# A recurrence with a highway layer on one core: bv by channel halves, weights scaled on ScalarE, a shorter ramp, and a new list of all operations

## The chip, the cores and the metric

The kernel runs on one core of a Trainium2 chip. That core has five engines with their own instruction queues: TensorE (PE, with PEld for its weight loads), VectorE (DVE), ScalarE (ACT), GpSimd (POOL) and SyncE (SP), which here issues the transfers. 16 DMA engines move data between the chip's main memory and the on-chip buffers. The metric is device time in microseconds, the median of several executions. The profile describes one execution, and its times count from the start of that execution's span.

## The reference

The input has 4 sequences of 6336 tokens with 256 channels, 25344 tokens in all. A gated recurrence over time is followed by a highway layer with two 256x256 weights:

```python
sig = 1.0 / (1.0 + np.exp(-f_logit))
f = lower_bound + (1.0 - lower_bound) * sig
i = 1.0 - f
for t in range(S):                      # per sequence
    h = f[:, t] * h + i[:, t] * x[:, t]
    y[:, t] = h
H = np.maximum(y @ w_h, 0.0)
T = 1.0 / (1.0 + np.exp(-(y @ w_t + b_t)))
out = T * H + (1.0 - T) * y
```

All data come and go as float32: 52 MB are read and 26 MB written.

## The kernel before

The tokens are cut into 28 units, in blocks of 128 tokens: two units of 2 blocks, one of 4, twenty-three of 8, one of 4 and one of 2. Each unit goes through these steps; a letter names each step in the list of operations, with the unit's number and a part behind it (`s4.1` is the scan of unit 4, channel half 1), a `v` puts the step on VectorE that else runs on ScalarE or GpSimd, and a number after a colon is the buffer it takes.

- `l` and `x` load the gate's logits and the input (SP issues them).
- `u` makes 1 - sigmoid of the logits on ScalarE (L256), with tokens on partitions.
- `b` multiplies u and x into `bv`, mostly on GpSimd (L264). A piece covers two block pairs and all 256 channels, so a unit of 8 blocks has two pieces of 1024 elements per partition.
- `i` and `p` turn u and bv with TensorE so that channels stand on partitions (uT at L271, bT at L291), once for each half of 128 channels.
- `f` scales uT into the gate (L282 on ScalarE, L280 on VectorE), and `s` is the scan over the tokens on VectorE (L308): y = f*y + bT, in which each unit goes on from the last token of the one before.
- `z` and `g` are the two weight products (L320 and L114), `t` the sigmoid on ScalarE (L333), `d` a combination of g and y on VectorE (L337), `e` the product d*t on GpSimd or VectorE (L343).
- `o` turns y and d back and adds them on TensorE (L365, L366), `c` copies the result out of the accumulator (L378 on ScalarE, L376 on VectorE) and `w` stores it.

The signs are arranged so that y is kept scaled by a constant per channel; the weights are multiplied by that constant `cc` once, in the ramp, and an identity is taken off w_h. In the kernel before VectorE does all this (`WT` at L217, `WH` at L231 and L233), with a negated scaled identity, `ndiag` (L212), that it makes first. `k` steps are filler matmuls on zeros, mostly in the ramp.

What sets the order is the list itself: it is walked once, each step's instructions are appended to the queue of their engine, and they stay in that order there. Buffers are taken by the number in the list: five accumulator tiles, four output tiles, and rings for l, x, u, bv, f, y, d and t. Loads and stores stand in one queue, SP's, and a store that waits for its copy holds back the loads behind it. `shared` adds a wait: a GpSimd product waits for the VectorE product (or the VectorE constant work) that stands ahead of it in the list.

Of the kernel before, what the change touches and what calls it, by code (L numbers as in the profile page):

```python
# [19 lines left out]
def kernel(  # L20
# [21 lines left out]
    parts = [2] * 2 + [4] + [8] * 23 + [4] + [2]  # L42
    units, at = [], 0
    for n, nb in enumerate(parts):
        units.append((nb, at, {2: (0, 1), 4: (0, 1, 2), 8: (0, 2, 4)}[nb], (0, 2048) if 7 <= n <= 21 else {2: (0, 256, 512), 4: (0, 512, 1024), 8: (0, 1024, 1536, 2048)}[nb]))
# [4 lines left out]
k*3:1 i0.1:0 f0.1:0 dg i1.0:1 b1.0v:1 f1.0:1 k*3:1 k*3:a0 p0.1:1 s0.1:0 i0.0:0 u2:0 f0.0v:0 p0.0:1 s0.0 x6:1 l7:2  # L50
k*3:a0 WT pb:0 k*3:a1 i2.0:0 p1.0:1 f2.0:0 WH k*3:1 s1.0:1 i2.1:0 b2.1v:0 g0.0:1 b2.0 i1.1:1 z0.1:2 f2.1:1 cb f1.1v:2
z0.0:0 g0.1:a0 p1.1:1 t0.0:0 d0.0:0 k*3:1 d0.1 p2.0:0 s1.1 k*3:0 e0.0v z1.1:1 p2.1:1 t0.1 u3:0 l8:3 g1.1:0 x7:2 s2.0:2
e0.1 d1.1:1 b3.0:0 z1.0:2 t1.0:0 i3.1:0 f3.1:0 o0.0:0 g1.0:2 c0.0:0 s2.1 d1.0 b3.1v g2.1:2 i3.0:0 d2.1:0 p3.1*3:1 t1.1
e1.1 e1.0 k*2:0 w0.0 u4:1 z2.0:1 f3.0:1 z2.1:0 b4.0:1 s3.1:0 p3.0:0 o1.0:2 t2.1:0 u27:0 b4.1 c1.0:1 s3.0 w1.0 x8:3
i4.0:1 g2.0:0 f4.0:0 d2.0 i4.1:1 p4.0:0 l9:1 x9:4 l11:4 t2.0 u5:2 e2.1v e2.0v z3.0:0 g3.1:1 b27.0:0 z3.1:2 s4.0:1
p4.1:0 f4.1:1 i5.0:1 t3.0:0 t3.1 d3.1:1 b5.0:2 g3.0:0 f5.0:0 s4.1 o2.0:1 u6:1 b5.1 c2.0:2 d3.0 w2.0 i5.1:1 x11:0 e3.2
g4.1:2 p5.0:0 d4.1:0 b6.0:1 f5.1:1 s5.0:2 z4.1:0 t4.1:1 p5.1:1 b6.1 u7:2 e3.1 s5.1 l10:0 z4.0:1 t4.0 g4.0:0 i6.0:0
e3.0v p6.0:1 d4.0 o3.0:1 e4.2 b7.0:2 f6.0:0 s6.0:3 e4.0v i6.1:0 b7.1 u8:3 f6.1:1 o3.1:0 c3.0:0 c3.1:1 w3.1 w3.0 g5.0:2
# [15 lines left out]
p15.1:1 s15.1 c12.1:1 b17.1:2 f16.0:2 z14.1:0 z14.0:2 p16.0:0 s16.0:1 c12.0:3 t14.1:1 t14.0 g14.0:1 d14.0 i16.1:1
w11.1 l19:1 u18:3 x18:0 b17.0 e14.0 g15.1:0 d15.1:2 z15.0:2 i17.1:0 x19:3 f16.1:0 b18.0:3 p16.1:1 f17.1:1 b18.1 l20:2
s16.1 o13.1:1 t15.0:0 p17.0:0 g15.0:0 w12.1 d15.0 c13.1:0 u19:1 b19.1:1 o13.0:2 p17.1:1 z15.1:1 c13.0:2 z16.0:0
s17.1:2 t15.1 t16.0:1 z16.1:2 s17.0 g16.0:1 w13.1 t16.1 i18.0:1 d16.0:0 g16.1:0 o14.0:2 i18.1:0 f18.0:0 d16.1 e15.0v
o14.1:1 p18.0:1 s18.0:3 u20:2 w12.0 z17.0:0 c14.0:0 c14.1:1 f18.1:1 g17.0:2 d17.0:1 z17.1:1 b19.0 t17.0:0 i19.1:0
f19.1:0 p18.1:1 o15.1:0 w13.0 s18.1 t17.1 x20:1 i19.0:0 l21:0 g17.1:2 e16.0 d17.1 o15.0:1 f19.0:2 b20.0:2 b20.1
p19.1:0 x21:2 w14.0 i20.1:1 c15.1:2 g18.1:0 w14.1 s19.1:0 c15.0:3 z18.0:1 f20.1:1 l22:1 o16.0:2 d18.1:2 w15.1 u21:1  # L80
t18.0:1 p19.0:0 c16.0:0 i20.0:1 g18.0:0 s19.0 f20.0:0 o16.1:1 c16.1:1 z18.1:2 i21.1:0 b21.1:1 p20.0:1 t18.1 e17.0v
d18.0 o17.0:1 w15.0 z19.1:0 b21.0 f21.1:2 g19.0:2 s20.0:1 x22:0 d19.0:0 p20.1:0 s20.1 c17.0:2 t19.1:0 o17.1:1 u22:2
e18.0 z19.0:0 g19.1:2 b22.1:2 c17.1:3 t19.0 i21.0:1 d19.1 e19.0 i22.0:0 b22.0 f21.0:0 g20.1:1 z20.1:0 l23:2 w16.0
# [12 lines left out]
t27.0:1 o25.3:1 d26.1 g27.0:a0 w23.1 z27.1:a1 w24.1 w24.0 e26.0 c25.2:0 e26.1v o26.0:2 o26.1:0 d27.0:0 g27.1:a0 d27.1
w25.0 c25.3 t27.1 e27.0 e27.1v o27.0:1 c27.0v:1 c26.0:2 o27.1:a0 c26.1 w25.1 w26.0 w27.0 c27.1:3 w27.1
# [110 lines left out]

    def do_dg(slot):
        for h in range(NH):  # L210
            pin(nc.vector.tensor_scalar(diag[:, h], ident_h, cc[:, h:h + 1], None, op0=ALU.mult))
            last = pin(nc.vector.tensor_scalar(ndiag[:, h], ident_h, ncc[:, h:h + 1], None, op0=ALU.mult))  # L212
        shared(last, False)

    def do_WT(slot):
        for h in range(NH):
            last = pin(nc.vector.tensor_scalar(w_sb[:, 1, h], w_raw[:, 1, h], cc[:, h:h + 1], None, op0=ALU.mult))  # L217
# [83 lines left out]
    def half(n, key, h):  # L301
        return st[n][key][:, h * tokens(n):(h + 1) * tokens(n)]
# [120 lines left out]
```

## Time and profile before

| what | us |
|---|---|
| median of 3 runs | 208.47 |
| lowest and highest | 208.37, 209.25 |
| span of the profiled execution | 206.1 |
| VectorE busy | 194.5 |
| TensorE busy | 192.6 |
| ScalarE busy | 191.9 |
| GpSimd busy | 173.8 |
| first bv on VectorE | 5.52 |
| first bv on GpSimd | 12.91 |

The span is the profiled execution's own time; the runs are timed around it, which accounts for the 2.4 us between the span and the median. Busy time is the sum of an engine's instructions, overlaps counted once; waiting and issuing do not count. A row of the timeline gives start, duration, engine, line, operation, the tiles written and read, the number of instructions merged into the row (x2), and in brackets the idle time ahead of it with what ended it. In the rows of groups the mean duration of one instruction stands in ns.

### The profile page before, as it was taken

The page shows a single profiled execution, that of the slowest core. Times are in us where ns is not written, and L with a number is a line of the kernel's source. Part 1 is how long each engine was busy: PE and PEld are TensorE (multiplying, and loading weights), DVE is VectorE, ACT ScalarE, POOL GpSimd, SP SyncE. Part 2 cuts the span into 40 slices and gives each one's busy share as a digit, 9 for nine tenths or more (in the row PEclk, how much of TensorE's full clock was granted, in tenths as well). Part 3 has the DMA queues.
Part 4 walks back from the last instruction along what each step waited for, and adds up shares of the span by engine and source line. Part 5 has one row for each costly group of instructions (what it writes and reads, how often), then busy time and mean ns, then how long its engine had stood idle before and what let it go on. Part 6 is the DMA issues. An engine that isn't in the chain of part 4 may idle for free.

```text
span 206.1 us, 4635 instructions
## 1 busy us (share of the span) xinstructions
PE 192.6 (93%) x1837; PEld 133.8 (65%) x1837; DVE 194.5 (94%) x159; ACT 191.9 (93%) x192; POOL 173.8 (84%) x93
## 2 busy tenths in 40 slices
PE   7798799799998999999999999999999999999991
PEld 2366465566685776676577576677758758776770
DVE  0899999999999999999899999999999999999972
ACT  4369999999999999999999999999999999999891
POOL 3036989789979997999999999799899999998840
PEclk9999999999999999999999999999999999999997
DMA  6999999999999999999999999999999999725396
GB/s 196 370 424 422 411 418 423 409 423 417 414 423 408 429 417 426 423 420 413 425 424 416 433 411 417 429 415 418 407 422 422 414 392 378 286 104 204 138 382 248
DMA packets 16125, 78.68 MB, mean 382 GB/s; under 512 B 1764, under 2 KB 2536, under 8 KB 10216
## 3 DMA queue, kind: packets, MB, share of 16 engines
q1 hardware_dynamic: 16096, 78.39, 93.6%
q8 instruction: 14, 0.23, 0.4%
q14 instruction: 7, 0.06, 0.1%
q10 hardware_dynamic: 8, 0.00, 0.0%
HBM read 52.43 MB, written 25.95 MB: 380 GB/s over the span
## 4 chain that ended last, share of the span: by engine, by line
PE 53%; ACT 14%; DMA 13%; DVE 10%; issue 6%; POOL 2%; SPq 1%; ACTq 0%; DVEq 0%; POOLq 0%
DMA x<-in_x_dram 9%; DVE y L308 8%; PE op L366 7%; PE bT L291 7%; PE op L365 7%; PE g L320 7%; PE z L320 6%; PE uT L271 6%; PE g L114 6%; PE z L114 6%; ACT o L378 4%; ACT f L282 4%; DMA out_dram<-o 4%; ACT t L333 3%; POOL bv L264 2%
## 5 line engine op out<-in xcount | busy, mean ns | idle before, releaser
L264 POOL TENSOR_TENSOR bv<-u,x 128x1024 bf16<-128x1024 f16 (+1 forms) x49 | 100.9, 2085 | 16.9 <-DVE bt L207 10.7
L308 DVE TENSOR_TENSOR_SCAN y<-f,y,bT 128x1024 bf16<-128x1024 f16 (+5 forms) x54 | 106.8, 1989 | 0.2 <-PE bT L291 0.2
L343 POOL TENSOR_TENSOR d<-d,t 128x512 bf16<-128x512 bf16 (+3 forms) x33 | 73.3, 2234 | 9.6 <-DVE d L343 4.2
L337 DVE SCALAR_TENSOR_TENSOR d<-y,ncc,g 128x1024 bf16<-128x1024 bf16 (+2 forms) x56 | 63.1, 1137 | 1.5 <-PE g L320 1.0
L333 ACT ACTIVATE t<-z,bt 128x1024 bf16<-128x1024 f32 (+2 forms) x56 | 58.9, 1088 | 1.3 <-PE z L114 0.7
L282 ACT ACTIVATE f<-uT,ncc 128x1024 f16<-128x1024 f16 (+2 forms) x51 | 55.4, 1098 | 3.4 <-PE uT L271 2.2
L378 ACT COPY o<-op 128x1024 f32<-128x1024 f32 (+2 forms) x55 | 52.1, 984 | 2.4 <-PE op L366 1.6
L256 ACT ACTIVATE u<-l 128x2048 f16<-128x2048 f32 (+2 forms) x28 | 49.8, 1781 | 2.8 <-DMA l<-in_f_logit_dram 2.7
L366 PE MATMUL op<-ident_b,d 128*128 128x128 bf16 x396 | 49.5, 219 | 0.6 <-DVE d L343 0.6
L365 PE MATMUL op<-diag,y 128*128 128x128 f16 x396 | 49.7, 219 | 0.1
L366 PEld LDWEIGHTS <-d 128*128 128x128 bf16 x396 | 44.0, 113 | 3.2 <-DVE d L343 0.7
L365 PEld LDWEIGHTS <-y 128*128 128x128 bf16 x396 | 44.2, 113 | 1.7
L320 PE MATMUL g<-y,w_sb 128*128 128x512 bf16 (+1 forms) x112 | 39.5, 367 | 0.9 <-DVE d L337 0.7
L320 PE MATMUL z<-y,w_sb 128*128 128x512 bf16 (+1 forms) x112 | 39.3, 367 | 0.4 <-ACT o L378 0.4
L291 PE MATMUL bT<-ident_f,bv 128*128 128x128 f32 x198 | 31.8, 277 | 4.3 <-DVE y L308 2.6
L114 PE MATMUL z<-y,w_sb 128*128 128x512 bf16 x92 | 34.9, 379 | 0.0
L114 PE MATMUL g<-y,w_sb 128*128 128x512 bf16 x92 | 34.9, 379 | 0.0
L320 PEld LDWEIGHTS <-w_sb 128*128 128x128 f16 x224 | 21.6, 98 | 17.5 <-issue 0.9
L271 PEld LDWEIGHTS <-u 128*128 128x128 f16 x396 | 26.3, 98 | 10.2 <-issue 2.6
L271 PE MATMUL uT<-ident_h,u 128*128 128x128 f16 x396 | 31.2, 220 | 1.6 <-DVE y L308 0.8
L291 PEld LDWEIGHTS bT<-ident_f,bv 128*128 128x128 f32 x198 | 22.4, 141 | 12.3 <-ACT f L282 3.0
L114 PEld LDWEIGHTS <-w_sb 128*128 128x128 f16 x184 | 18.0, 98 | 16.7 <-issue 1.8
(39 smaller groups left out, 58.7 us busy)
## 6 DMA issues: line engine op xcount, KB each, us to landing
out_dram<-o SPq DMA_DIRECT2D x48, 512.0 KB, 7.7
l<-in_f_logit_dram SPq DMA_DIRECT2D x23, 1024.0 KB, 12.0
x<-in_x_dram SPq DMA_DIRECT2D x23, 1024.0 KB, 13.4
l<-in_f_logit_dram SPq DMA_DIRECT2D x2, 512.0 KB, 7.5
x<-in_x_dram SPq DMA_DIRECT2D x2, 512.0 KB, 7.2
l<-in_f_logit_dram SPq DMA_DIRECT2D x3, 256.0 KB, 2.9
x<-in_x_dram SPq DMA_DIRECT2D x3, 256.0 KB, 3.9
out_dram<-o SPq DMA_DIRECT2D x2, 256.0 KB, 16.3
```

The lines of the kernel that those rows point to most:

```text
L114: return pe.add_instruction(mybir.InstMatmult(name=nc.get_next_instruction_name(), start_tensor_calc=start, stop_tensor_calc=stop, tile_si ...
L264: shared(pin(e.tensor_mul(st[n]["bv"][:, a:c].rearrange("p k d j -> p k j d"), st[n]["u"][:, 2 * a:2 * c].rearrange("p (k j) d -> p k j d" ...
L271: pin(nc.tensor.transpose(uT[:, j * P:(j + 1) * P], st[n]["u"][:, j, h * P:(h + 1) * P], ident_h))
L282: pin(nc.scalar.activation(to, of, AF.Identity, scale=ncc[:, h:h + 1], bias=1.0))
L291: pin(nc.tensor.transpose(words[:, k:k + g * (P - 1) + 1:g], pair, ident_f))
L308: pin(nc.vector.tensor_tensor_scan(y[:, c:e], st[n]["f", h][:, c:e], st[n]["bT", h][:, c:e], 0.0 if fresh else carry[h], op0=ALU.mult, op1 ...
L320: pin(nc.tensor.matmul(p[:, a:e], w, half(n, "y", ki)[:, a:e], start=ki == 0, stop=ki == NH - 1))
L333: pin(nc.scalar.activation(half(n, "t", m), st[n]["z", m][:, :tokens(n)], AF.Sigmoid, bias=bt[:, m:m + 1]))
L337: pin(nc.vector.scalar_tensor_tensor(half(n, "d", m), half(n, "y", m), ncc[:, m:m + 1], st[n]["g", m][:, :tokens(n)], op0=ALU.mult, op1=AL ...
L343: shared(pin(e.tensor_mul(st[n]["d"][:, a:c], st[n]["d"][:, a:c], st[n]["t"][:, a:c])), not eng)
L365: pin(nc.tensor.matmul(o, half(n, "y", h)[:, cols], diag[:, h], start=True, stop=False))
L366: pin(nc.tensor.matmul(o, half(n, "d", h)[:, cols], ident_b, start=False, stop=True))
```

## The change

The units are cut anew: two of 2 blocks, three of 4, twenty-two of 8, one of 4, one of 2, which is 29. A piece of bv now covers one channel half and all blocks of its unit, in a tile of its own, so that the turning of that half waits for that piece alone. y has a tile for each half, from a ring of eight. In the ramp GpSimd subtracts the identity from w_h in place (`IW`), and ScalarE scales both weights (`WHa`, `WTa`, two instructions of 256 elements each); `ndiag` is gone. The list of all operations is new from the first token to the last.

```diff
-    parts = [2] * 2 + [4] + [8] * 23 + [4] + [2]
+    parts = [2] * 2 + [4] * 3 + [8] * 22 + [4] + [2]
...
-l1:0 l0:1 x0:0 x1:1 k*3:a0 l2:2 wt wh x2:2 l3:3 x3:3 l4:4 pc:0 x4:4 u0:0 l27:1 l5:5 b0.0v:0 x27:0 x5:5 u1:1 cc l6:0
+l0:0 k*3:a0 x0:0 k*2:0 pc:0 k*3:1 l1:1 wh wt u0:0 x1:1 u1:1 l2:2 l3:3 b0.1v:0 b0.0v:1 cc dg k*2:a0 i0.0:1 i0.1:0 f0.1:0
...
+    def do_IW(slot):
+        for h in range(NH):
+            own = w_raw[:, 0, h, h * P:(h + 1) * P]
+            last = pin(nc.gpsimd.tensor_sub(own, own, ident_f))
+        shared(last, True)
...
-            pin(nc.vector.tensor_scalar(diag[:, h], ident_h, cc[:, h:h + 1], None, op0=ALU.mult))
-            last = pin(nc.vector.tensor_scalar(ndiag[:, h], ident_h, ncc[:, h:h + 1], None, op0=ALU.mult))
+            last = pin(nc.vector.tensor_scalar(diag[:, h], ident_h, cc[:, h:h + 1], None, op0=ALU.mult))
...
+    def scaled(k, act):
+        for h in range(NH):
+            if act:
+                pin(nc.scalar.activation(w_sb[:, k, h], w_raw[:, k, h], AF.Copy, scale=cc[:, h:h + 1]))
...
-    def do_b(n, k, eng, slot):
-        if "bv" not in st[n]:
-            st[n]["bv"] = sb([P, NB // 2, D, 2], BF16, "bv", slot)
-        a, c = units[n][2][k:k + 2]
+    def do_b(n, h, eng, slot):
+        nb = units[n][0]
+        bv = sb([P, NB // 2, P, 2], BF16, "bv", slot)
+        own = slice(h * P, (h + 1) * P)
         e = nc.vector if eng else nc.gpsimd
-        shared(pin(e.tensor_mul(st[n]["bv"][:, a:c].rearrange("p k d j -> p k j d"),
-                                st[n]["u"][:, 2 * a:2 * c].rearrange("p (k j) d -> p k j d", j=2),
-                                st[n]["x"][:, 2 * a:2 * c].rearrange("p (k j) d -> p k j d", j=2))), not eng)
+        shared(pin(e.tensor_mul(bv[:, :nb // 2].rearrange("p k d j -> p k j d"),
+                                st[n]["u"][:, :nb, own].rearrange("p (k j) d -> p k j d", j=2),
+                                st[n]["x"][:, :nb, own].rearrange("p (k j) d -> p k j d", j=2))), not eng)
+        st[n]["bv", h] = bv
...
     def do_s(n, h, eng, slot):
-        flat(n, "y", "y", slot)
+        st[n]["y", h] = sb([P, NB * P], BF16, "y", slot)
```

The list shows at three places in the ramp what it moves. First VectorE's queue from its first bv on, before:

```order
L264 TENSOR_TENSOR bv<-u,x 128x2x256
L200 TENSOR_SCALAR ncc<-lbT 128x2
L201 TENSOR_SCALAR cc<-lbT 128x2
L211 TENSOR_SCALAR diag<-ident_h,cc 128x128
L212 TENSOR_SCALAR ndiag<-ident_h,ncc 128x128
L211 TENSOR_SCALAR diag<-ident_h,cc 128x128
L212 TENSOR_SCALAR ndiag<-ident_h,ncc 128x128
L264 TENSOR_TENSOR bv<-u,x 128x2x256
L308 SCALAR_TENSOR_TENSOR y<-f,bT 128x256
L280 TENSOR_SCALAR f<-uT,ncc 128x256
L308 SCALAR_TENSOR_TENSOR y<-f,bT 128x256
L217 TENSOR_SCALAR w_sb<-w_raw,cc 128x256 x2
```

The same place after the change (the scan is named by its form, y is what it writes):

```order
L276 TENSOR_TENSOR bv<-u,x 128x2x128 x2
L200 TENSOR_SCALAR ncc<-lbT 128x2
L201 TENSOR_SCALAR cc<-lbT 128x2
L217 TENSOR_SCALAR diag<-ident_h,cc 128x128 x2
L293 TENSOR_SCALAR f<-uT,ncc 128x256
L323 SCALAR_TENSOR_TENSOR y<-f,bT 128x256 x2
L293 TENSOR_SCALAR f<-uT,ncc 128x256
L207 COPY bt<-tbT 128x2
L276 TENSOR_TENSOR bv<-u,x 128x2x128
L352 SCALAR_TENSOR_TENSOR d<-y,ncc,g 128x256
```

The products of bv are half as wide, ndiag and the weights are gone, and the first d stands where the weights stood. ScalarE's queue in the ramp, before:

```order
L256 ACTIVATE u<-l 128x512 x2
L282 ACTIVATE f<-uT,ncc 128x256 x2
L256 ACTIVATE u<-l 128x1024
L282 ACTIVATE f<-uT,ncc 128x512 x2
L333 ACTIVATE t<-z,bt 128x256 x2
L256 ACTIVATE u<-l 128x2048
```

and after:

```order
L268 ACTIVATE u<-l 128x512 x2
L295 ACTIVATE f<-uT,ncc 128x256
L228 ACTIVATE w_sb<-w_raw,cc 128x256 x4
L295 ACTIVATE f<-uT,ncc 128x256
L348 ACTIVATE t<-z,bt 128x256
L268 ACTIVATE u<-l 128x1024
```

The four scalings of the weights stand between the first two f that ScalarE makes. SP's queue from the start, before (l is the logits, x the input, w_raw the two weights as they come):

```order
L244 DMA l<-in_f_logit_dram 128x512 x2
L244 DMA x<-in_x_dram 128x512 x2
L244 DMA l<-in_f_logit_dram 128x1024
L187 DMA w_raw<-in_moe_w_t_dram 128x2x256
L190 DMA w_raw<-in_moe_w_h_dram 128x2x256
L244 DMA x<-in_x_dram 128x1024
```

and after:

```order
L256 DMA l<-in_f_logit_dram 128x512
L256 DMA x<-in_x_dram 128x512
L256 DMA l<-in_f_logit_dram 128x512
L190 DMA w_raw<-in_moe_w_h_dram 128x2x256
L187 DMA w_raw<-in_moe_w_t_dram 128x2x256
L256 DMA x<-in_x_dram 128x512
```

x of unit 0 moves from third to second place, both weights move ahead of x of unit 1, and w_h comes ahead of w_t. Later in the list loads use rings of six buffers throughout, where before l used three and x four after the ramp, and one of the four output tiles keeps its store from unit 17 until unit 25.

More of the change, by code (lines that the diff above doesn't have):

```diff
@@ L54 @@
[L54 to L58, printed above, removed]
@@ L74 @@
[L74 to L78, printed above, removed]
@@ L79 @@
[L79 to L83, printed above, removed]
@@ new lines @@
+p15.1:0 i16.0:1 e13.0 f16.0:2 d14.0:2 w12.1 g14.1:1 o12.0:2 s15.1:1 d14.1 u17:3 w11.1 i16.1:1 b16.1:0 p16.0:0 s16.0:6 f16.1:0
+b17.0:2 c12.0:3 z14.0:0 t14.0 b17.1:3 e14.0 o13.0:1 p16.1:1 c13.0:2 o13.1:2 l19:2 c13.1:0 s16.1:7 i17.0:0 g15.1:0 x18:0
+z15.0:1 p17.0:1 f17.0:1 d15.1:1 w10.0 z16.0:2 i17.1:0 g16.1:0 s17.0:2 w13.1 l20:3 x19:1 w12.0 t15.0:2 t16.0:1 g15.0:1 z15.1:2
+d16.1:0 g16.0:0 p17.1:1 d15.0 f17.1:2 b18.0:5 u19:0 b18.1:4 d16.0 i19.0:0 t15.1 o14.1:1 z16.1:2 s17.1:3 f19.0:0 c14.1:1 t16.1
```

119 lines of the change are left out of this document (66 added, 53 removed).

## The prediction

> **What bounds the kernel now.** I read the busy totals first, then a table of stages, then the timelines of the ramp. The page's busy times:
>
> ```profile
> span 206.1 us, 4635 instructions
> PE 192.6 (93%) x1837; PEld 133.8 (65%) x1837; DVE 194.5 (94%) x159; ACT 191.9 (93%) x192; POOL 173.8 (84%) x93
> ```
>
> Nothing stands out: three engines are within two percent of each other. The table of stages says where the missing 6% lies:
>
> ```profile
> 0.00:12.00 12.00, 9.76 (x40) 4.13 (x41) 6.40 (x19) 5.27 (x8) 1.62 (x11) 1.00 0.86 303
> 12.00:32.00 20.00, 18.03 (x160) 12.12 (x160) 20.00 (x23) 19.07 (x21) 14.94 (x11) 1.00 1.02 419
> 32.00:172.00 140.00, 135.19 (x1324) 95.77 (x1323) 139.43 (x93) 139.58 (x129) 132.87 (x58) 1.00 1.02 417
> 172.00:190.00 18.00, 18.00 (x179) 12.66 (x177) 18.00 (x12) 17.30 (x20) 17.31 (x11) 1.00 0.61 242
> 190.00:206.10 16.10, 11.63 (x143) 9.10 (x140) 10.66 (x16) 10.68 (x18) 7.01 (x6) 0.94 0.63 246
> ```
>
> The columns are PE, PEld, DVE, ACT and POOL busy, the granted clock, the DMA share and GB/s. From 32 to 172 us VectorE lacks 0.57 us of 140 and ScalarE 0.42. So the program lasts as long as VectorE's head start (when its dense work begins), plus its work, plus the drain. The DMA engines are full there too, but the share falls to 0.61 after 172 us, when the loads are over and the engines are not, so I take them as a constraint on the order and not as the end. What a new list can win in the middle is half a microsecond; the ramp and the drain are where time can go.
>
> VectorE's ramp before, from its timeline (start, duration, line, form, idle before):
>
> ```profile
> 5.52 0.73 DVE L264 TENSOR_TENSOR bv<-u,x 128x512 bf16<-128x512 f16 x1 [4.39 <-DMA x<-in_x_dram]
> ...
> 6.99 0.28 DVE L212 TENSOR_SCALAR ndiag<-ident_h,ncc 128x128 f32<-128x128 f16 x1
> ...
> 9.86 0.59 DVE L217 TENSOR_SCALAR w_sb<-w_raw,cc 128x256 f16<-128x256 f32 x2
> 10.36 0.35 DVE L231 SCALAR_TENSOR_TENSOR w_sb<-w_raw,cc,ndiag 128x128 f16<-128x128 f32 x1
> 10.62 0.28 DVE L233 TENSOR_SCALAR w_sb<-w_raw,cc 128x128 f16<-128x128 f32 x1
> ...
> 12.06 0.71 DVE L264 TENSOR_TENSOR bv<-u,x 128x512 bf16<-128x512 f16 x1
> 12.67 0.14 DVE L207 COPY bt<-tbT 128x2 f32<-128x2 f32 x1
> 12.73 0.47 DVE L280 TENSOR_SCALAR f<-uT,ncc 128x256 f16<-128x256 f16 x1
> 13.12 0.89 DVE L337 SCALAR_TENSOR_TENSOR d<-y,ncc,g 128x256 bf16<-128x256 bf16 x2
> 13.94 0.74 DVE L308 TENSOR_TENSOR_SCAN y<-f,y,bT 128x256 bf16<-128x256 f16 x1
> 14.59 0.27 DVE L343 TENSOR_TENSOR d<-d,t 128x256 bf16<-128x256 bf16 x1
> ...
> 16.40 1.27 DVE L308 TENSOR_TENSOR_SCAN y<-f,y,bT 128x512 bf16<-128x512 f16 x1
> 17.59 0.46 DVE L337 SCALAR_TENSOR_TENSOR d<-y,ncc,g 128x256 bf16<-128x256 bf16 x1
> 17.96 1.75 DVE L264 TENSOR_TENSOR bv<-u,x 128x1024 bf16<-128x1024 f16 x1
> ...
> 24.83 0.72 DVE L337 SCALAR_TENSOR_TENSOR d<-y,ncc,g 128x512 bf16<-128x512 bf16 x1
> 25.47 0.78 DVE L343 TENSOR_TENSOR d<-d,t 128x512 bf16<-128x512 bf16 x2
> 26.17 2.34 DVE L308 TENSOR_TENSOR_SCAN y<-f,y,bT 128x1024 bf16<-128x1024 f16 x1
> 28.43 1.25 DVE L337 SCALAR_TENSOR_TENSOR d<-y,ncc,g 128x1024 bf16<-128x1024 bf16 x1
> 29.61 2.34 DVE L308 TENSOR_TENSOR_SCAN y<-f,y,bT 128x1024 bf16<-128x1024 f16 x1
> 31.86 1.25 DVE L337 SCALAR_TENSOR_TENSOR d<-y,ncc,g 128x1024 bf16<-128x1024 bf16 x1
> ```
>
> Records overlap by some 0.08 us, so I count start to start: scans 0.65, 1.19 and 2.26 us for 256, 512 and 1024 tokens; d 0.37, 0.64 and 1.18; e 0.19 and 0.35 (256, 512); f of 256 0.39; a bv of 512 elements 0.61 (12.06 to 12.67). At 31.86 us the scans of units 0 to 4, 3072 tokens, are done.
>
> **The change, part by part.** Arrival of data first. The chain of waits gives two landings by transfer, ScalarE's timeline two more:
>
> ```profile
> 1.63 3.79 DMA x<-in_x_dram
> 6.82 14.43 DMA x<-in_x_dram
> ```
>
> ```profile
> 4.12 1.15 ACT L256 ACTIVATE u<-l 128x512 f16<-128x512 f32 x2 [1.27 <-DMA l<-in_f_logit_dram]
> 6.39 0.84 ACT L282 ACTIVATE f<-uT,ncc 128x256 f16<-128x256 f16 x2 [1.12 <-DVE cc L201]
> 8.67 1.06 ACT L256 ACTIVATE u<-l 128x1024 f16<-128x1024 f32 x1 [1.44 <-DMA l<-in_f_logit_dram]
> 11.22 0.69 ACT L282 ACTIVATE f<-uT,ncc 128x512 f16<-128x512 f16 x1 [1.49 <-PE uT L271]
> ```
>
> One transfer queue serves SP's order, so arrival goes by bytes: 0.52 MB (two pieces of 256 KB) by 4.1 us, 0.79 by 5.4, 1.57 by 8.6, 6.82 (x of unit 4) by 21.25; the last two make 5.25 MB in 12.6 us, 416 GB/s. In the new SP order x0 is second (4.1), l1 third (5.4), wh (1.05 MB) by 6.5 and wt by 7.5 (between the rows), x1 at 8.6, later than before since both weights now stand ahead of it; l2 9.9, l3 11.1, x2 12.4, x3 13.7, x4 16.2, x5 21.25.
>
> VectorE then walks so. The first bv starts at 4.2 and not 5.52 us: minus 1.3. The two halves of unit 0 (256 elements each; between half of 0.61 and all of it; I take 0.33, as the rows scale with size), ncc, cc, two diag and f0.0 end at 5.9. The scan s0.1 needs f0.1, which on ScalarE stands behind the u of unit 1 (5.4 plus 0.57, half of the x2 row) and takes 0.42: 6.5, a new wait of 0.6. Two scans and f1.0 end at 8.25; bv of unit 1 waits for x1 until 8.6, 0.35 more. From there bv, d0.1, bv, s1.1, e, s1.0, d0.0, an f of 512 (0.65, between 0.39 and the 1.2 of twice its size and d's rate), e and d1.0 reach 12.7, two bv of unit 2 13.9. Then come six scans of 512 (7.1), d of 256 and three of 512 (2.3), e's of units 1 to 3 (1.4) and s5.1: 27.0. What they wait for is there: GpSimd makes the four bv of units 3 and 4 from 13.9 to 18.7 at 1.2 each, and s5.1, at 24.8, needs x5 (21.25) and one bv of 2.2. d4.1 and s5.0 end at 29.9, with a tenth for hand-overs at 30.0, where the same 3072 tokens stood at 31.86: **1.8 us earlier**. The parts: 1.3 from the start; 0.2 less work on VectorE (the weights and ndiag, 2x0.28 + 0.59 + 2x0.35 + 2x0.28 less overlap, leave, 1.8; three more e, more bv pieces, split scans and the f of 512 come back); 0.9 of new waits against it; the remaining 1.2 is what stood idle or blocked in the ramp before.
>
> ScalarE takes four weight scalings. None is in the trace; 256 elements of f take 0.42 and 512 of u 0.57, so 0.28 to 0.42 each, 0.33 taken, 1.3 us in all. They lie between f0.1 (6.4) and f1.1, where ScalarE before waited 1.12, 1.44 and 1.49 us in three places, so they cost nothing unless that cover goes. Ahead of the first stand wh and GpSimd's two subtractions of 128 elements, some 0.4 each (below the 0.67 of 256), done at 7.3; its w_sb follows at 7.7, g0.1 at 8.2, before VectorE asks for it at 8.9. If this ran 0.7 later, d0.1 would be late next.
>
> GpSimd's rows, by form:
>
> ```profile
> L264 POOL TENSOR_TENSOR bv<-u,x 128x1024 bf16<-128x1024 f16 x45 | 96.2, 2165 | 5.4 <-DVE d L343 3.0 <-PE bT L291 1.3 <-DMA x<-in_x_dram 0.9
> L343 POOL TENSOR_TENSOR d<-d,t 128x1024 bf16<-128x1024 bf16 x2 | 4.3, 2155 | 0.7 <-DVE d L343 0.7
> L264 POOL TENSOR_TENSOR bv<-u,x 128x512 bf16<-128x512 f16 x4 | 4.7, 1192 | 11.5 <-DVE bt L207 10.7 <-DVE d L343 0.8
> L343 POOL TENSOR_TENSOR d<-d,t 128x256 bf16<-128x256 bf16 x4 | 2.6, 672 | 4.0 <-DVE d L337 1.8 <-DVE bv L264 1.3 <-DVE d L343 0.9
> ```
>
> A bv by channel half has eight runs of 128 elements instead of four of 256. Four runs cost 2165 and one run (the d row) 2155 ns, so a run is nearly free: 44 more such instructions at zero to 10 ns extra, taken as nothing. Its other bound is that each run costs what an instruction does at its start, 2x1192 - 2165 = 219 ns, a rival below. What it gives: the first half's transposes wait for one GpSimd instruction and not for two, 2.1 us less latency, which buys slack and no busy time. The y tiles by halves only free buffers sooner. TensorE loses six filler matmuls; it has gaps, nothing follows.
>
> After the point reached both lists hold the same VectorE work: 21 units of eight blocks, one of four, one of two, three f of 1024, two copies, and 14 e's (more of 512) for 13: within 0.1 us by the rows. ScalarE, too, has the same u, f, t and o of those units left. Middle and drain I price at nothing, between a gain of 2 us and a loss of 3 (below). The sum: span 206.1 - 1.8 = 204.3 us. The median of 208.47 stands 2.4 above the profiled span, hence **206.7 us**.
>
> **Rivals.** (1) The list also closes what is left: 0.57 us in the middle, and of the 5.4 us that VectorE is idle after 190 us perhaps 1.3. That makes 204.9. For it: the halves give slack; against: the drain's steps are the same chain of small units.
>
> (2) ScalarE gives the gain back. It is as dense as VectorE from 32 us on; if u's wait for data as long as before, its 1.3 us of scaling come on top: 208.0.
>
> (3) Slower: VectorE collides with GpSimd. The bv row at 17.96 takes 1.75 us where two of 0.61 would do, because GpSimd was in an instruction:
>
> ```profile
> 16.40 2.14 POOL L264 TENSOR_TENSOR bv<-u,x 128x1024 bf16<-128x1024 f16 x1 [0.72 <-DMA x<-in_x_dram]
> ```
>
> This ends at 18.54; 1.2 us later is 19.7, just when the VectorE row ends. So VectorE stood still some 0.5 us. VectorE now has 27 products of two such operands (bv and e) for 20. Seven more at 0.5 us are 3.5: 210.2. It decides from 0.4 us each on. Against it: the list makes GpSimd wait for the VectorE product ahead of it, and the e rows above ran at 0.35 and 0.19, unblocked. The Trainium skill (SBUF — State Buffer, "Who interferes with whom") says that a VectorE instruction with two SBUF inputs and a GpSimd instruction that reads SBUF exclude each other, and that the one issued first keeps the port to its end; by that rule, which this pair of rows bears out, the worst case is a whole GpSimd instruction per product.
>
> (4) Slower: each run of the new bv costs a start on GpSimd, up to 4 x 0.22 = 0.88 us an instruction. Of GpSimd's 32 idle us, 10.4 lie in the first row of the stages and 9.1 in the last; the other 12.8 allow 0.29 us for each of the 44. Above that it decides: at 0.5 us GpSimd lengthens the span by 22 - 12.8 = 9 us, 215.9. The pair 2165 and 2155 speaks against it.
>
> (5) Slower: stores. One of four output tiles is held from unit 17 to unit 25, so three turn over while a store takes
>
> ```profile
> out_dram<-o SPq DMA_DIRECT2D x48, 512.0 KB, 7.7
> ```
>
> 7.7 us to land. A copy that waits stops ScalarE; 3 us in all make 209.7, and from 2.8 on it is slower. Against it: a unit, with two stores, is 2x2.26 + 2x1.18 = 6.9 us of VectorE, so three tiles turn over in 10.
>
> **How the numbers follow.** Forecast 0.50 (its own range 205.4 to 207.9), rival 1 0.12, rival 2 0.16, rival 3 0.11, rival 4 0.06, rival 5 0.05. Half a percent, 1.04 us, is about what a measurement of this kernel can tell from no change: 207.43 and 209.51 are the marks. Faster is 0.45 of the forecast and rival 1, 0.57; same 0.05 of the forecast and most of rival 2, 0.19; the rest is slower, 0.24. The range from 204.4 to 210.2 leaves out rival 4, half of rival 3 and the far ends.
>
> **What would show it.** Right: VectorE's first bv near 4.2 us, the scans of 3072 tokens done near 30.1, weight rows on ScalarE near 7 us, GpSimd's bv at 2.16 us, 0.5 to 1 us idle on VectorE between 32 and 172 us. Wrong: bv rows on GpSimd over 2.3 us, e or bv rows on VectorE far over their size, copies that wait for stores, or VectorE idle over 2 us in the middle.

## The result and the profile after

The kernel after takes 218.46 us in the median of 4 runs (217.48 to 219.46), the kernel before beside it 208.86 (208.37 to 210.78). The ratio is 1.0455, with a 95% interval of 1.0392 to 1.0517: 9.6 us slower, where 206.7 was forecast and 210.2 was the end of the range. The ratios leave out single executions that fell in a slower state, so a ratio can differ a little from that of the medians given beside it. The experiments below were measured in three groups on two chips, each group beside runs of the kernel before (208.31, 208.16 and 208.30 us), and every ratio is against those.

The page after, busy times:

```profile
span 217.7 us, 4632 instructions
PE 195.3 (90%) x1803; PEld 134.3 (62%) x1831; DVE 195.8 (90%) x163; ACT 194.5 (89%) x200; POOL 176.6 (81%) x98
```

The span is 11.6 us longer, 2 us more than the medians differ, because the profiled execution is the slowest of the four (219.46). VectorE works 195.8 us where it worked 194.5, so it idles 21.9 us where it idled 11.6: 10.3 of the 11.6 us are waits, 1.3 are more busy time. The table of stages, with the columns of the prediction's, says when:

```profile
0.00:12.00 12.00, 10.47 (x50) 4.74 (x50) 6.62 (x19) 7.40 (x14) 2.48 (x13) 1.00 0.82 302
12.00:32.00 20.00, 18.18 (x146) 11.20 (x148) 19.84 (x26) 18.82 (x24) 13.25 (x9) 1.00 1.02 420
32.00:172.00 140.00, 127.90 (x1235) 90.91 (x1253) 133.03 (x89) 130.66 (x119) 125.00 (x55) 0.99 0.98 379
172.00:190.00 18.00, 15.73 (x132) 10.32 (x133) 14.34 (x10) 16.39 (x16) 14.71 (x7) 0.91 0.92 358
190.00:217.70 27.70, 22.97 (x252) 17.14 (x252) 21.98 (x23) 21.19 (x31) 21.16 (x17) 0.99 0.67 258
```

From 32 to 172 us VectorE lacks 6.97 us (before 0.57), and the last column falls from 417 to 379 GB/s. Between 172 and 190 us, where before the loads were over, transfers still run at 358.

The ramp did become shorter. Its end on VectorE's timeline after:

```profile
28.67 2.35 DVE L323 TENSOR_TENSOR_SCAN y<-f,y,bT 128x1024 bf16<-128x1024 f16 x1 [0.16 <-PE bT L304]
30.93 1.38 DVE L352 SCALAR_TENSOR_TENSOR d<-y,ncc,g 128x512 bf16<-128x512 bf16 x2
```

At 30.93 us the scans of 3072 tokens are done, which before was at 31.86. By the ends of the later scans, which the two lists place differently between the other steps, the lead is not lost for good until 114 us: 6144 tokens are done 1.6 us later than before, 7168 tokens 3.6 us earlier, 14336 tokens 1.1 us earlier (113.9 against 114.9), but 15360 tokens 5.7 us later (127.5 against 121.8) and 18432 tokens 8.0 us later.

**Where it went.** The page's row of GB/s in forty equal slices, before:

```profile
GB/s 196 370 424 422 411 418 423 409 423 417 414 423 408 429 417 426 423 420 413 425 424 416 433 411 417 429 415 418 407 422 422 414 392 378 286 104 204 138 382 248
```

and after:

```profile
GB/s 193 384 425 417 420 420 419 413 422 353 286 318 425 427 416 423 372 420 387 319 422 362 324 358 280 357 425 420 424 356 320 425 398 347 271 290 112 366 264 277
```

Before, the transfers stand at 407 to 433 GB/s for thirty slices in a row; after, the same height is broken from the tenth slice (49 us) on. Two wide windows of the same columns as the stages put numbers on it, before:

```profile
10.00:50.00 40.00, 36.07 (x313) 23.91 (x313) 39.97 (x40) 37.76 (x38) 31.18 (x20) 1.00 1.02 418
50.00:140.00 90.00, 87.62 (x870) 62.32 (x868) 89.43 (x60) 89.58 (x83) 85.79 (x36) 1.00 1.02 420
```

after:

```profile
10.00:50.00 40.00, 37.16 (x318) 23.78 (x321) 39.84 (x44) 38.82 (x43) 30.05 (x18) 1.00 1.02 419
50.00:140.00 90.00, 81.83 (x789) 58.44 (x800) 84.98 (x55) 83.17 (x77) 78.86 (x34) 0.98 0.97 366
```

Until 50 us both move the same. From 50 to 140 us the kernel after moves 90 x 0.366 = 32.9 MB where before it was 37.8; the missing 4.9 MB take 11.6 us at 420 GB/s, which is as much as the span grew. That is a hint and not a proof: in this window VectorE itself loses only 4.5 us against before, and the other waits come later. The experiments have to show the cause.

Why the transfers ran dry shows SP's queue after (start, duration, line, what is issued):

```profile
39.34 0.34 SPq L397 DMA_DIRECT2D out_dram<-o  x1
39.79 0.87 SPq L256 DMA_DIRECT2D x<-in_x_dram  x1
41.80 0.33 SPq L256 DMA_DIRECT2D l<-in_f_logit_dram  x1
54.73 0.34 SPq L397 DMA_DIRECT2D out_dram<-o  x1
55.17 0.38 SPq L256 DMA_DIRECT2D x<-in_x_dram  x1
55.60 0.79 SPq L256 DMA_DIRECT2D l<-in_f_logit_dram  x1
```

By the list, the issues from 39.34 on are w4.0, x10, l12, w5.0, x11 and l13. SP stands 12.6 us in front of the store of unit 5, whose copy is not made yet (11.6 of them are put down to that copy), and with it stand x11 and l13, whose buffers are free. What was queued before lands meanwhile (l12 at 55.43), and the slices 353, 286 and 318 follow. There are more such holds, at 72, 119, 147 and 166 us, 9 to 12 us each. How much SP waits in all is no sign of it. Its waits for copies before (in total, times, longest):

```profile
SPq L382 <- ACT o L378: 110.2, 37, 7.5
```

and after:

```profile
SPq L397 <- ACT o L393: 113.6, 30, 11.6
```

The sums are alike; single holds grew longer, and loads with free buffers stand behind them. The bill comes later, as waits for data that land at the last moment. The waits after, by engine (in total, times, longest; two views, ScalarE's and GpSimd's):

```profile
ACT u L268 <- DMA l<-in_f_logit_dram: 8.0, 6, 2.4
ACT o L393 <- DMA out_dram<-o: 3.2, 3, 2.7
```

```profile
POOL bv L276 <- DMA x<-in_x_dram: 7.7, 8, 1.9
```

The same three were 2.7, 0.4 and 0.9 us before. VectorE sees them one or two steps on. Its longest wait after, and ahead of it on ScalarE's timeline a copy that waits for a store:

```profile
111.54 2.35 DVE L323 TENSOR_TENSOR_SCAN y<-f,y,bT 128x1024 bf16<-128x1024 f16 x1 [0.51 <-PE bT L304]
117.66 1.28 DVE L352 SCALAR_TENSOR_TENSOR d<-y,ncc,g 128x1024 bf16<-128x1024 bf16 x1 [3.77 <-PE g L115]
```

```profile
112.73 1.01 ACT L393 COPY o<-op 128x1024 f32<-128x1024 f32 x1 [2.72 <-DMA out_dram<-o]
113.64 1.12 ACT L348 ACTIVATE t<-z,bt 128x1024 bf16<-128x1024 f32 x1
```

The chain of waits after has the store (start, duration):

```profile
99.80 12.91 DMA out_dram<-o
```

It was issued at 99.80 and landed at 112.71, and with it the output tile came free; the copy freed the accumulator, TensorE's g followed, and d with it. So the row names TensorE, and the cause is a transfer three steps back.

### The profile page after: what moved, and what is told of

Same layout as the page of the kernel before. It is cut to its first block, busy times and chain, and to the rows that moved or that the text cites. A ratio compares the mean times of both kernels' runs of the same rounds, so it can differ in the third digit from the quotient of the medians.

```text
span 217.7 us, 4632 instructions
## 1 busy us (share of the span) xinstructions
PE 195.3 (90%) x1803; PEld 134.3 (62%) x1831; DVE 195.8 (90%) x163; ACT 194.5 (89%) x200; POOL 176.6 (81%) x98
## 2 busy tenths in 40 slices
DMA packets 16413, 78.68 MB, mean 361 GB/s; under 512 B 1796, under 2 KB 2568, under 8 KB 10760
## 4 chain that ended last, share of the span: by engine, by line
PE 32%; DMA 27%; ACT 15%; issue 10%; DVE 9%; POOL 4%; SPq 1%; ACTq 0%; DVEq 0%; POOLq 0%
DMA out_dram<-o 16%; DVE y L323 7%; DMA l<-in_f_logit_dram 6%; DMA x<-in_x_dram 5%; PE op L381 4%; PE op L380 4%; ACT t L348 4%; ACT o L393 4%; PE z L335 4%; PE g L335 4%; ACT u L268 4%; PE bT L304 3%; PE uT L284 3%; POOL bv L276 3%; ACT f L295 3%
## 5 line engine op out<-in xcount | busy, mean ns | idle before, releaser
L276 POOL TENSOR_TENSOR bv<-u,x 128x1024 bf16<-128x1024 f16 (+2 forms) x52 | 102.8, 1997 | 26.8 <-DMA x<-in_x_dram 7.7
L348 ACT ACTIVATE t<-z,bt 128x1024 bf16<-128x1024 f32 (+2 forms) x58 | 57.1, 1007 | 1.9 <-PE z L115 1.4
L268 ACT ACTIVATE u<-l 128x2048 f16<-128x2048 f32 (+2 forms) x29 | 48.7, 1680 | 8.0 <-DMA l<-in_f_logit_dram 8.0
L393 ACT COPY o<-op 128x1024 f32<-128x1024 f32 (+2 forms) x55 | 49.9, 929 | 6.4 <-DMA out_dram<-o 3.2
L295 ACT ACTIVATE f<-uT,ncc 128x1024 f16<-128x1024 f16 (+2 forms) x52 | 53.0, 1030 | 2.4 <-PE uT L284 2.2
L335 PE MATMUL z<-y,w_sb 128*128 128x512 bf16 (+1 forms) x115 | 40.7, 373 | 3.8 <-ACT o L393 2.1
L335 PE MATMUL g<-y,w_sb 128*128 128x512 bf16 (+1 forms) x113 | 40.3, 377 | 2.3 <-ACT o L393 1.5
L284 PEld LDWEIGHTS <-u 128*128 128x128 f16 x396 | 26.9, 99 | 11.9 <-issue 4.9
L115 PE MATMUL z<-y,w_sb 128*128 128x512 bf16 x78 | 30.2, 387 | 0.0
L115 PE MATMUL g<-y,w_sb 128*128 128x512 bf16 x76 | 29.6, 389 | 0.1
```

Source lines behind the costliest of these rows:

```text
L115: return pe.add_instruction(mybir.InstMatmult(name=nc.get_next_instruction_name(), start_tensor_calc=start, stop_tensor_calc=stop, tile_si ...
L276: shared(pin(e.tensor_mul(bv[:, :nb // 2].rearrange("p k d j -> p k j d"), st[n]["u"][:, :nb, own].rearrange("p (k j) d -> p k j d", j=2), ...
L284: pin(nc.tensor.transpose(uT[:, j * P:(j + 1) * P], st[n]["u"][:, j, h * P:(h + 1) * P], ident_h))
L295: pin(nc.scalar.activation(to, of, AF.Identity, scale=ncc[:, h:h + 1], bias=1.0))
L335: pin(nc.tensor.matmul(p[:, a:e], w, half(n, "y", ki)[:, a:e], start=ki == 0, stop=ki == NH - 1))
L348: pin(nc.scalar.activation(half(n, "t", m), st[n]["z", m][:, :tokens(n)], AF.Sigmoid, bias=bt[:, m:m + 1]))
```

## The experiments

Three theories stood at first. A: transfers (loads stand behind stores that wait for copies, the DMA engines run dry, and copies wait for tiles whose stores land late). B: a part of the change is dear in itself. C: VectorE and GpSimd collide in their products. In the second group A is sharpened to D, transfers are a second bound beside VectorE, and L stands against it: the new list lets the engines wait for each other more, whatever the transfers do. In the list pieces below only SP's steps are shown (l and x load, w stores).

**The parts without the new list.** The kernel before, with its own units and its own list, takes the halves of bv and y, the subtraction on GpSimd and the scalings on ScalarE:

```diff
-k*3:a0 WT pb:0 k*3:a1 i2.0:0 p1.0:1 f2.0:0 WH k*3:1
+k*3:a0 WTa pb:0 k*3:a1 i2.0:0 p1.0:1 f2.0:0 IW WHa k*3:1
```

> The units and the list of before, with the parts of the change alone: bv by channel halves, y by halves, GpSimd subtracting the identity, ScalarE scaling both weights. Theory A (transfers: in the new list loads stand behind stores that wait for their copies, the DMA engines run dry, loads come late; and copies wait for an output tile whose store lands late): the parts are harmless, 207.5 to 209.5 us. Theory B (the parts are dear: eight short runs on GpSimd, weights on ScalarE): 213 us or more. Theory C (VectorE's products collide with GpSimd's instructions, 27 for 20): up to 211, as two of the small bv pieces are new here.

Measured: 208.67 us, ratio 1.0017 (0.9993 to 1.0042). Its rows by form have GpSimd's bv as in both other kernels:

```profile
L275 POOL TENSOR_TENSOR bv<-u,x 128x1024 bf16<-128x1024 f16 x45 | 96.3, 2170 | 4.8 <-DVE d L357 2.5 <-PE bT L303 1.3 <-PE uT L283 0.8
```

The parts cost nothing and bring nothing. B falls; the loss lies in the new list or in the new cut of the units, which this run does not have.

**Six output tiles.** The list of the kernel after, with the tiles dealt anew to six slots:

```diff
-    w_raw = sb([P, 2, NH, D], FP32, "w_raw")
+    w_raw = pool.tile([P, 2, NH, D], FP32, tag="o5", name="w_raw")
```

> After, with six output tiles instead of four (the raw weights share the sixth), each given to the copy that needs one next; the order of all operations is the same. Theory A: copies no longer wait for stores; the 3.8 us stall of VectorE at 113 us, which hangs on such a copy, goes, loads still come late: 212 to 216 us. B and C: no change, 217 to 219.

Measured: 216.33 us, ratio 1.0417 (1.0342 to 1.0493). The time lies between what A (up to 216) and what B and C (from 217) expected. No copy waits for a store any more, but the intervals of this ratio and of the change's own overlap: tiles alone are worth 0.8 us by the two ratios and 2.1 by the medians, and are not the main cause. The transfers still run short:

```profile
50.00:140.00 90.00, 82.44 (x810) 58.90 (x821) 88.57 (x58) 85.90 (x80) 81.67 (x35) 1.00 0.97 380
```

The 3.6 MB less than before take 8.6 us at 420 GB/s; this span is 8.3 us longer than before.

**SP's steps in another order, first try.** Stores right behind their copies, loads 14 us of VectorE work ahead of their use, with four tiles, and with six:

```diff
-x2 x3 l4 x4 l5 x5 l6 x6 l7 l8 x7 l9 l10 x8 w2.0 w0.0 w1.0 x9 l11 w4.0 x10 l12 w5.0 x11
+x2 x5 x3 l4 l6 x4 l5 x6 l7 w0.0 l8 x7 l9 x8 w1.0 w2.0 l10 x9 w4.0 l11 x10 w3.0 x11 l12
```

> After, with SP's queue alone in another order: each store right behind its copy, each load 14 us of VectorE's work ahead of its first use (the first 12 loads and the last stores as they were); the order on PE, VectorE, ScalarE and GpSimd is the same. Theory A: most of the loss comes back, 206 to 211 us, and SP waits no more than 8 us at a time for a copy. B and C: 216 to 219.

> Both of the two before together. Theory A: the least time of the four, 205 to 209 us. B and C: 216 to 219.

Measured: 217.44 us, ratio 1.0441 (1.0382 to 1.05), and with six tiles 216.86, 1.0435 (1.0383 to 1.0487). What A expected did not come: both times lie where B and C had them, but the windows of the second kernel tell why:

```profile
10.00:50.00 40.00, 33.43 (x270) 21.21 (x274) 36.44 (x41) 34.08 (x39) 25.60 (x16) 0.96 1.01 408
50.00:140.00 90.00, 86.26 (x854) 61.89 (x865) 89.98 (x63) 90.00 (x84) 84.66 (x37) 1.00 1.00 397
140.00:170.00 30.00, 26.31 (x263) 18.86 (x265) 27.61 (x20) 27.30 (x26) 26.48 (x11) 1.00 1.00 386
```

VectorE lost 3.4 us before 50 us, since the edit had also moved the ramp's loads: a u waited 3.83 us for l5. Then it was dense for 90 us, denser than before, while the transfers ran at 397 and not 420; 2.1 MB stayed behind, taken from loads that at first landed 3 to 10 us early. At 148.54 us that stock was used up (x22 landed 0.13 us ahead of its use), and VectorE stalled. A dry stretch of the transfers can thus be paid 60 us later, at a place that has nothing wrong with it.

**Half of the stored bytes.** The same edit in the kernel before and in the kernel after; waits, lists and tiles stay as they are:

```diff
+        m = max((j1 - j0) // 2, 1)
-        pin(nc.sync.dma_start(rows(out, n, j0, j1), st[n]["o", j0][:, :j1 - j0]))
+        pin(nc.sync.dma_start(rows(out, n, j0, j1)[:, :m], st[n]["o", j0][:, :m]))
```

> Every store of the kernel before writes the first half of its token rows only, so that about 13 of 78.7 MB are not moved; all waits, copies and the order stay (half of the output is left out). The slices of the kernel before show 409 to 429 GB/s from the second to the thirty-first, and VectorE lacks 0.57 of 140 us there: two limits at one height. Theory D (transfers are a second bound beside VectorE): VectorE still takes what it took, so 206.5 to 208.5 us, 0 to 2 us less than before, with transfers well under 400 GB/s in the middle. Were transfers the only bound, it would fall by ten us or more. Theory L (the lists differ in how tightly the engines wait for each other; transfers do not matter): 208.3, no change.

> The same halving of the stored bytes in the kernel after, with its list, its queue and its four output tiles untouched (half of the output is left out). Theory D: the time lost in dry stretches of the queue can be made up, since transfers now need only some 156 us at 420 GB/s; loads land early again and VectorE is dense: 205 to 210 us, 8 to 13 us less than after. Theory L: 215 to 219, as after, since each wait between the engines is still there.

Measured: 207.75 us, ratio 0.9978 (0.9964 to 0.9992), for the kernel before; 208.55 us, ratio 1.0016 (0.9998 to 1.0034), for the kernel after. The windows of the latter:

```profile
50.00:140.00 90.00, 85.71 (x835) 61.08 (x848) 89.98 (x60) 88.94 (x82) 85.00 (x37) 1.00 0.91 337
```

With its own list, queue and four tiles, the kernel after loses nearly all of its excess (4.55% to 0.16%) once there are fewer bytes to move, and VectorE is dense. SP still stands in front of its stores as long as before the edit (116.6 us in all, 11.8 at the longest), but the transfers catch up. L expected 215 to 219 and falls. Shorter stores also land earlier and free the four output tiles sooner (no copy waits for a store here), so this run alone does not part late loads from scarce tiles; the runs below do. The window of the kernel before with the same edit:

```profile
50.00:140.00 90.00, 86.86 (x859) 62.41 (x870) 89.72 (x61) 89.74 (x83) 85.90 (x36) 1.00 0.96 356
```

It gains only 0.2%: there VectorE holds the time, and the transfers, though full, were just in step with it.

**Stores on another queue.** ScalarE issues them, SP has loads alone:

```diff
-        pin(nc.sync.dma_start(rows(out, n, j0, j1), st[n]["o", j0][:, :j1 - j0]))
+        pin(nc.scalar.dma_start(rows(out, n, j0, j1), st[n]["o", j0][:, :j1 - j0]))
```

> The kernel after, with its stores issued by ScalarE, behind its own copies, instead of by SP; loads alone are left on SP's queue, so that none stands behind a store that waits. Theory D: no dry stretch of 10 us on the queue, 400 GB/s and more from 50 to 140 us, and a time of 209 to 215 us (each of some 50 issues may cost ScalarE up to 0.1 us, and the output tiles are still four). Theory L: 216 to 220.

Measured: 246.05 us, ratio 1.1791 (1.1707 to 1.1875), far outside what either theory expected. One row of ScalarE's waits tells it:

```profile
ACT o L393 <- DMA out_dram<-o: 27.9, 12, 4.4
```

Loads, no longer held back by anything but their buffers, keep the transfers at 400 to 426 GB/s from 10 to 100 us, and the stores behind that backlog come home late; twelve copies wait for one of four tiles, and ScalarE with them. TensorE's granted clock was 0.90 from 50 to 140 us there; what that added was not separated. The Trainium skill (DMA: Bandwidth & Descriptors, "Issuing engines are not separate DMA queues") says that transfers started by different engines run on the same 16 DMA engines and interleave; this run fits that in its rate, at 419 GB/s from 10 to 50 us with one issuer as with two. What SP's mixed queue did badly in the kernel after, rationing loads against stores, is thus needed, at least with four tiles; six were not tried with this queue.

**SP's steps, second try.** As the first, but the loads up to x9 and the stores among them keep their places, the loads come 18 us of VectorE work ahead, and there are six tiles:

```diff
-x9 l11 w4.0 x10 l12 w5.0 x11 l13 w6.1 w5.1 x12 w3.0 x13 w6.0 l14 x14 w7.0 w7.1 l15 l16
+x9 w4.0 l11 x10 x11 w3.0 l12 x12 l13 w6.1 w5.0 w5.1 x13 w6.0 l14 x14 l15 w7.0 w7.1 w8.1 x15 l16
```

> The kernel after with six output tiles and SP's list rewritten behind the ninth x load: each store right behind its copy, each load 18 us of VectorE work ahead of its use or, later, right behind the last reader of its buffer; the ramp's loads keep their order. Theory D: the two earlier rewrites lost 3.4 us in the ramp, which is kept here, and let the transfers run dry at 40 to 90 us with a lead of 14 us; with both mended the bytes moved by 150 us come within 1 MB of the kernel before (61.4 MB), and the time is 205.5 to 210 us. Theory L: 213 to 217, as the other rewrites, with stalls of VectorE at 150 to 180 us although loads have landed 1 us or more ahead of use.

Measured: 207.80 us, ratio 0.9982 (0.9966 to 0.9999). All other engines keep the list of the kernel after, and its loss is gone. So the units' new cut is not the cause either, nor is C, since all 27 products of VectorE keep their places. The window:

```profile
50.00:140.00 90.00, 86.19 (x847) 61.75 (x859) 89.98 (x60) 90.00 (x84) 85.53 (x37) 1.00 1.02 419
```

Transfers are at their height and VectorE lacks 0.02 us of 90. In this stretch loads land 1.8 to 8.5 us ahead of use.

**The same with four tiles.**

Tiles dealt to four slots again, and the weights' buffer its own:

```diff
-    w_raw = pool.tile([P, 2, NH, D], FP32, tag="o5", name="w_raw")
+    w_raw = sb([P, 2, NH, D], FP32, "w_raw")
```

> SP's rewritten list (stores right behind their copies, loads 18 us of VectorE work ahead) with the four output tiles of the kernel after. Theory D1 (SP's list alone is the cause): 207.5 to 209 us, within 1 us of the same list with six tiles (207.8). Theory D2 (four tiles are also too few for this list, since a store needs 9 to 13 us to land when the transfers are full): 210 to 214, with copies that wait for a store's landing for some 2 to 5 us in sum.

Measured: 211.69 us, ratio 1.0156 (1.0117 to 1.0195), 1.7% or 3.6 us over the six tiles. The window:

```profile
50.00:140.00 90.00, 82.33 (x802) 58.62 (x815) 86.83 (x57) 85.74 (x80) 82.76 (x36) 1.00 1.02 419
```

The transfers are full and the loads in time (1 to 9 us early), yet VectorE lacks 3.17 us: with this order the tiles are a second cause of their own, as D2 had it. Only 1.4 us of waiting copies is put down to stores by name, less than the expected 2 to 5; the rest wears other names further down the chain, and its course was not followed.

**Stores alone, loads alone.** Two kernels with six tiles that share the move of the second try between them. First only the stores move:

```diff
-x9 l11 w4.0 x10 l12 w5.0 x11 l13 w6.1 w5.1 x12 w3.0 x13 w6.0 l14 x14 w7.0 w7.1 l15 l16
+x9 w4.0 w3.0 w6.1 l11 w5.0 x10 w5.1 l12 x11 w6.0 l13 x12 x13 w7.0 l14 x14 w7.1 w8.1 w8.0 l15
```

> Six output tiles, and only the stores moved, right behind their copies; the loads keep the places of the kernel after. If late stores are what matters: 208 to 210 us. If loads that come to SP too late are what matters (they stand behind a store that waits for its copy, while nothing else is queued): 213 to 217, near the 216.3 of six tiles alone, with x used within 0.2 us of its landing in many units.

Measured: 236.41 us, ratio 1.1321 (1.1248 to 1.1395), far above both of the ranges expected. Stores that come to SP early make SP stand in front of them early, with the late loads behind: it waits 152.2 us for copies, where it waits 110.0 with six tiles alone. In the page's slices the transfers fall to 80 and 237 GB/s at 47 to 58 us. Its waits, over all engines:

```profile
POOL bv L276 <- DMA x<-in_x_dram: 20.7, 6, 6.5
ACT u L268 <- DMA l<-in_f_logit_dram: 16.4, 14, 4.2
```

Then only the loads move:

```diff
-x9 l11 w4.0 x10 l12 w5.0 x11 l13 w6.1 w5.1 x12 w3.0 x13 w6.0 l14 x14 w7.0 w7.1 l15 l16
+x9 l11 x10 x11 l12 x12 l13 w4.0 w5.0 x13 l14 w6.1 w5.1 w3.0 x14 l15 w6.0 w7.0 x15 w7.1 l16
```

> The counterpart: six output tiles, and only the loads moved, to 18 us of VectorE work ahead of their use; the stores keep the places of the kernel after. If the loads' places matter: 207.5 to 210 us. If the late stores matter: 213 to 217.

Measured: 207.26 us, ratio 0.9945 (0.992 to 0.997). Its windows:

```profile
10.00:50.00 40.00, 37.17 (x313) 23.58 (x316) 39.85 (x45) 38.65 (x43) 29.43 (x18) 1.00 1.02 419
50.00:140.00 90.00, 86.18 (x847) 61.73 (x858) 89.98 (x60) 90.00 (x84) 85.52 (x37) 1.00 1.02 420
140.00:170.00 30.00, 28.88 (x302) 21.50 (x305) 29.53 (x21) 29.86 (x28) 30.00 (x12) 1.00 1.02 420
```

Against six tiles alone the ratio falls from 1.0417 to 0.9945, some 9.8 us (9.1 by the medians), by nothing but the places and the order of the loads: every other step and every buffer number is the same. With six tiles the late stores were harmless, and putting them early did harm.

**Loads still earlier.** The second try with 22 us in place of 18:

```diff
-x9 w4.0 l11 x10 x11 w3.0 l12 x12 l13 w6.1 w5.0 w5.1 x13 w6.0 l14 x14 l15 w7.0 w7.1 w8.1 x15
+x9 w4.0 l11 x10 l12 x11 w3.0 x12 l13 w6.1 w5.0 w5.1 x13 l14 w6.0 x14 l15 w7.0 x15 w7.1 w8.1
```

> As the list with a lead of 18 us and six tiles (207.8 us, loads 2 to 7 us early), with a lead of 22 us. Theory D: VectorE alone bounds there, so loads that come still earlier bring nothing: 207.3 to 208.5 us; should stores now land too late behind the loads, copies wait for them and it is 209 or more.

Measured: 207.21 us, ratio 0.9946 (0.9919 to 0.9972), a tenth under the range that D gave. With the loads alone moved, this is the best here: 0.5% under the kernel before, 5% under the kernel after. The interval overlaps that of 18 us, which was measured on the other chip, so a gain from the longer lead is not shown.

## Why the prediction was wrong

**The bound: the step that failed.** "I take them as a constraint on the order and not as the end" dropped the transfers from the sum, though the row quoted for it had them at share 1.02 and 417 GB/s beside VectorE's 139.43 of 140 us. From that followed "Middle and drain I price at nothing, between a gain of 2 us and a loss of 3". The runs put this in its place: 78.68 MB at 420 GB/s are 187 us, and the first 12 us, at 302 GB/s, lose another 3.4. That leaves some 15 us of the span of 206.1 in which the transfers may rest, and the drain takes them, when loads are over and the engines are not. Before that a list has to hold two resources dense, not one. The kernel after rested them in the middle for what is worth 11.6 us, and paid: VectorE idles 6.4 us more than before from 32 to 172 us and 3.7 us more from there to 190. Two of the prediction's signs of being wrong came with it: a copy that waits for a store, and VectorE idle over 2 us in the middle. The cause is shown by the runs: with six tiles, moving the loads alone took 9.8 us away, and with four, halving the stored bytes took nearly all. The Trainium skill (DMA: Bandwidth & Descriptors, "Specifications") gives 435 GB/s as the ceiling of the ports by which transfers reach the on-chip buffers. The trace agrees: no slice of any run here is over 433, and the kernel before, at 407 to 433 in its middle, had little room left.

**Where the two lists were compared.** "After the point reached both lists hold the same VectorE work" holds well enough: the extra busy time of the whole span is 1.3 us, as much as one collided product below lost. What was not compared is SP's order: where each load stands behind a store, and when that store's copy is made.

**The ramp.** VectorE's first bv began at 4.23 us (4.2 forecast), and the weights stood on ScalarE at 7.67, in 1.72 us for the 1.3 forecast, with no one waiting. But the 3072 tokens were done at 30.93 and not 30.0: half of the 1.8 us. Two rows show the term that was mis-sized, ScalarE's and VectorE's:

```profile
6.41 0.63 ACT L268 ACTIVATE u<-l 128x512 f16<-128x512 f32 x1 [2.37 <-DMA l<-in_f_logit_dram]
```

```profile
6.58 0.48 DVE L293 TENSOR_SCALAR f<-uT,ncc 128x256 f16<-128x256 f16 x1 [0.67 <-PE uT L284]
7.56 1.26 DVE L323 TENSOR_TENSOR_SCAN y<-f,bT 128x256 bf16<-128x256 f16 x2 [0.49 <-PE bT L304]
```

The arrival by bytes put l1 at 5.4 us; its u began at 6.41. And the first scan, forecast at 6.5, began at 7.56, after two waits for TensorE that the walk did not have. With the loads in order this ramp is kept: the two best kernels are 1.0 to 1.1 us under the kernel before, which fits the 0.9 measured. The 2.4 us from span to median are partly spread between executions: where both are known for one execution they differ by 1.8 us (219.46 and 217.7 here), so the sum's last step was some 0.6 us too much.

**GpSimd's runs (rival 4).** Taken as free, and free: 2168 ns with eight runs of 128, 2165 with four of 256.

**Collisions (rival 3).** VectorE's longest product after, and GpSimd's row at the time:

```profile
73.31 2.60 DVE L358 TENSOR_TENSOR d<-d,t 128x2048 bf16<-128x2048 bf16 x1
```

```profile
70.56 4.27 POOL L276 TENSOR_TENSOR bv<-u,x 128x1024 bf16<-128x1024 f16 x2 [1.19 <-DMA x<-in_x_dram]
```

The product took 2.60 us, where the same form took 1.26 in the kernel before. GpSimd's second bv had begun 0.6 us ahead and ended at 74.83; 1.1 us later VectorE's row ends too, where the product takes 1.26 us when alone. The Trainium skill (SBUF — State Buffer, "Who interferes with whom") has the one that comes second wait for the whole instruction of the other, and these two rows agree within 0.2 us. The mechanism exists as priced, but with one full overlap in the middle; that is 1.3 us, not 3.5. It seems to have come from the transfers as well: the bv ahead of it had waited 1.19 us for x. In the second try of SP's steps the longest such row is 1.38 us.

**Stores and tiles (rival 5).** It had the side right and a place near the truth: a copy did wait for a store, at 113 us. Four tiles cost 3.6 us in the second try's order, where it said 3, but only 0.8 (2.1 by the medians) in the list that was forecast, so that the sizes are alike is in part luck. What it missed is the other direction, that a store which waits for its copy holds back the loads, worth nearly three times as much (9.8 us).

**Rivals 1 and 2.** The scalings on ScalarE were not what halved the ramp's gain. The middle that rival 1 hoped for did not come: with early loads VectorE lacks 0.02 us from 50 to 140, but over the stage from 32 to 172 us it is busy 139.51 us in the last run, where it was 139.43 before.

## What to carry to other kernels

When the busiest engine and the transfers are both full in the middle, a new order is priced on both: walk the issuing queue as an engine of its own, with each load's place behind each store and the time of that store's copy. Time that transfers rest there was not made up here, and showed up to some 60 us later as waits under other names; so look for slices below the steady height before looking at the stalls. Loads go well ahead of their use, but stores need their share, or tiles to wait in.

## What the runs showed of the hardware that was not expected

Loads and stores mixed hold 418 to 420 GB/s from 50 to 140 us in every kernel here whose loads were early enough, and a second issuer did not raise it (419 from 10 to 50 us). TensorE's granted clock, 1.00 throughout the middle before, fell to 0.91 from 172 to 190 us after, behind VectorE's stalls; no run here separates what that cost. Halving the stored bytes in the kernel before left the transfers at 356 GB/s from 50 to 140 us and gained 0.2%: the 64 GB/s more that it moves with whole stores hardly slow its engines.
